# A gated linear attention and two expert layers on one core: elementwise work of GpSimd moved to VectorE, the plan re-costed, heads moved by two queues, and another order of column blocks

## The chip, the core and the metric

One core of one Trainium2 chip runs the whole program. The metric is device microseconds of one execution; a kernel is timed by the median of several executions. The engines are named as the profile names them: PE is TensorE (PEld its weight loads), DVE is VectorE, ACT is ScalarE, POOL is GpSimd, SP is SyncE, which issues most DMAs.

## The reference

The program computes three layers in float32, one after the other:

```python
# attention, B=4, H=8, S=768, D=48
f = 1 / (1 + exp(-f_logit))
for t in range(S):
    state = f[:, :, t, :, None] * state + k[:, :, t] (x) v[:, :, t]   # outer product
    y[:, :, t] = q[:, :, t] @ state
# first expert layer, x: 3072 x 384, hidden width 1536
x = ((x @ w_a) * (x @ w_b)) @ w_out
# second expert layer: 4 experts of width 1024, weighted by normalised probabilities p
out = sum(p[:, e] * (max(x @ w1[e], 0) @ w2[e]) for e in range(4))
```

`w_a`, `w_b` and `w_out` arrive as 64-bit floats and are converted on the chip.

## The kernel before

The attention is done in chunks of 128 time steps: 24 steps, numbered s, for 6 chunks times 4 batches. The decay inside a chunk becomes a running product R (a scan on VectorE, L302). k is multiplied by R (L309) and q divided by it; for the first steps (`early`, s below `EARLY`, 12) the reciprocal is made on ScalarE as exp(-ln R) (L316, L317) and corrected once on VectorE and GpSimd (L318, L320, L322); for the others VectorE divides (L330, four per step) and multiplies (L331). Scores, outputs and state updates are small matmuls (L342, L355, L395, L402, L412). One half of the masked scores goes through VectorE (L371); the other, for early steps after the first four, through a ScalarE copy (L379) and a GpSimd select (L381). The output goes to the tile `xT` as a high and a low part (L432 on ScalarE, L436 on VectorE). Then the heads' last parts are moved to other partitions by six DMAs for each pair of steps (L451, all on SP).

The first expert layer runs over six token blocks of 512 columns and 12 column blocks f of 128 hidden units. A unit (block, f) is nine matmuls for a, nine for b (L500), the product, and the output matmuls: three plain ones for the first ten units (L545, `u < WHOLE`) and nine on split operands for the others (L552). Splitting means that a number is written as a rounded high part plus the low rest: ScalarE rounds (L525, L529), and GpSimd (units below `LATE`, 20) or VectorE subtracts (L532, L535). Each f needs its weights: a 768 KB load, five VectorE operations that turn 64-bit into 32-bit floats (L207, L226, L229, L232, L236), a ScalarE rounding (L250) and a GpSimd subtraction (L254); there are 18 such conversions, 12 for `w_a` and `w_b` and 6 for `w_out`. `ORDER` says which units come first: blocks 0 and 1 take f 0 to 7 each, then f 8 to 11 each. The attention for later blocks is woven in between.

This weaving is done when the program is built. Every operation of these two layers is a `Node` with an engine, a cost in us, what it waits for, and the buffers it takes and gives. A list planner walks through time by these costs and by a few lags (`STRETCH`, `HOP`, `DMA_LAG`) and writes the operations out; each engine then runs its own list strictly in that order. Until the first output matmul the planner fills planned idle time of PE with matmuls on a junk tile (L724). This whole part is called stage A here. Stage B, the second expert layer, follows (L758 and L776); its matmuls need nothing but the weights, which are loaded and split (L127, still on GpSimd), and the token blocks of stage A. `x2` of block 0 is split at the end of stage A (L632).

Of the kernel before, what the change touches and what calls it, by code (L numbers as in the profile page):

```python
# [27 lines left out]
NB = 512  # L28
NBLK = NT // NB
HB = 256  # L30
EARLY = 3 * B

SLOTS = 11
GRP = 2
NSUB = 2
ORDER = ((0, 8, 0), (0, 8, 1), (8, 12, 0), (8, 12, 1))
WHOLE = 10
LATE = 20

T_FIRST, STRETCH, SLACK, PATIENCE, HOP, DMA_LAG = 32.0, 1.15, 1.0, 0.3, 0.06, 2.0  # L40
PRINT = False
LIMIT = float(2.0 ** 60)

# [5 lines left out]
def gla_moe_moe_kernel(ctx: ExitStack, tc, qkf, vv, wab, wout, w12, probs, gq, gv, gp, out):  # L49
# [87 lines left out]
    def phase_a(actx):  # L137
# [30 lines left out]
        def w_plan(u):  # L168
# [24 lines left out]
            if not wide:  # L193
                if out_w:
                    n = Node("ACT", 0.9, lambda: nc.scalar.copy(out=dst(), in_=box["raw"]), [n_f] + guard, give=["k"])
                    w_out_n[f] = w_out_n[f + 1] = n
                    conv_mid.append(n)
                    return
                w, n_w, back = lambda: box["raw"], n_f, ["k"]
            else:  # L200
                seen = wseen[:, u]

                def shift():
                    t = keep.tile([128, 2, 2 * DM], F32, tag="k", name="cv")
# [13 lines left out]

                def exps():
                    return nc.scalar.activation(  # L220
                        out=box["sq"], in_=box["sq"], func=AF.Exp, scale=-64.0 / F64_ZERO, accum_out=seen[:, 1:2]
                    )

                n_s = Node("ACT", 2.2, lambda: (pin(sums()), pin(exps())), [n_f])
                n1 = Node("DVE", 0.8, shift, [n_f, conv_end[-2]], take=["k"])
                n2 = Node("DVE", 1.1, lambda: nc.vector.scalar_tensor_tensor(  # L226
                    out=box["val"].bitcast(U32), in0=box["high"], scalar=0xC0000000, in1=box["mag"].bitcast(U32),
                    op0=ALU.bitwise_and, op1=ALU.bitwise_or), [n1])
                n3 = Node("DVE", 0.72, lambda: nc.vector.tensor_scalar(  # L229
                    out=box["mag"].bitcast(U32), in0=box["val"].bitcast(U32), scalar1=0xFF800000, scalar2=None,  # L230
                    op0=ALU.bitwise_and), [n2])
                n4 = Node("DVE", 1.0, lambda: nc.vector.scalar_tensor_tensor(  # L232
                    out=box["mag"], in0=box["low"], scalar=float(2.0 ** -52), in1=box["mag"], op0=ALU.mult,
                    op1=ALU.mult), [n3])
                conv_mid.append(Node("free", 0.0, None, [n4, n_s], give=["k"]))
                n5 = Node("DVE", 1.0, lambda: nc.vector.tensor_tensor(  # L236
                    out=dst(), in0=box["mag"], in1=box["val"], op=ALU.add), [n4] + guard, give=["k"] if out_w else [])
                if out_w:
                    w_out_n[f] = w_out_n[f + 1] = n5
                    conv_end.append(n5)  # L240
                    return
                w, n_w, back = lambda: box["val"], n5, ["k"]

            def hi():
                if ff == 0:
# [5 lines left out]

            n6 = Node("ACT", 0.83, hi, [n_w] + ([w_n[0]] if ff == 1 else []),
                      take=["x"] if ff == 0 else [] if ff == 1 else ["w"])
            w_n[ff] = Node("POOL", 2.0, lambda: nc.gpsimd.tensor_tensor(  # L254
                out=box["t"][:, 1], in0=w(), in1=box["t"][:, 0].bitcast(F32), op=ALU.subtract), [n6], give=back)
            conv_end.append(w_n[ff])
            if not wide:
# [9 lines left out]
        def step_plan(s):  # L267
# [31 lines left out]
            def scan():  # L299
# [6 lines left out]
            end = slice(C - 1, C)  # L306
            n_max = Node("DVE", 0.15, lambda: dve.tensor_reduce(
                out=flags[:, s, 0:1], in_=t["R"][:, :, C - 1], axis=AX.X, op=ALU.max), [n_R])
            n_k = Node("POOL", 1.6, lambda: pool.tensor_tensor(out=t["k"], in0=t["k"], in1=t["R"], op=ALU.mult),  # L309
                       [n_R, loads["k"]])  # L310

            def new_pe():
# [2 lines left out]
            if early:  # L315
                n = Node("ACT", 0.63, lambda: act.activation(out=t["f"], in_=t["R"], func=AF.Ln), [n_R])  # L316
                n_p = Node("ACT", 0.63, lambda: act.activation(out=t["f"], in_=t["f"], func=AF.Exp, scale=-1.0), [n])  # L317
                n_q = Node("DVE", 1.0, lambda: dve.scalar_tensor_tensor(  # L318
                    out=t["q"], in0=t["q"], scalar=-1.0, in1=t["f"], op0=ALU.mult, op1=ALU.mult), [n_p, loads["q"]])
                n_r = Node("POOL", 1.65, lambda: pool.tensor_tensor(  # L320
                    out=t["R"], in0=t["R"], in1=t["f"], op=ALU.mult), [n_p, n_k, n_max])
                n_q = Node("DVE", 0.75, lambda: dve.scalar_tensor_tensor(  # L322
                    out=t["q"], in0=t["R"], scalar=-2.0, in1=t["q"], op0=ALU.add, op1=ALU.mult), [n_q, n_r])
# [120 lines left out]

            w = GRP * C
            if (o + C) % w == 0:
                def move():
                    z = xT[i].bitcast(F32)[:, :, :, o + C - w:o + C]
                    for h in (0, 64):
                        for kc in range(KC):  # L450
                            dma_i = dma.dma_start(  # L451
                                out=z[h + D:h + 64, :, kc], in_=z[h + 16 * kc:h + 16 * kc + 16, :, 3]
                            )
                            pin(dma_i)
                n_mv = Node("SP", 0.6, move, [lo_n[s], lo_n[s - 1]])
                for d in range(GRP):
                    mv_n[s - d] = n_mv
            if not last:
                def new_state():
                    t["new"] = at.tile([128, 4, D], F32, tag="st", name="st", bufs=B + 1)  # L460
# [22 lines left out]
            else:  # L483
                Node("free", 0.0, None, [n_o, n_pe], give=["st", "pe"])

        x_first, lo_n = {}, {}


        x2ps, x2n, rows, last_op, op_list = {}, {}, [], [None], [None] * 2
# [2 lines left out]
        def unit_plan(u, i, o, n, f, fs):  # L492
# [16 lines left out]
                return nc.scalar.copy(out=t["a"], in_=t["p", 0])  # L509
            n_ac = Node("ACT", 0.59 * narrow, copy_a, [n_a], take=["a"], give=["h"])  # L510
            n_b = state["b"] = Node("PE", cost, lambda: half(1), ready + [n_a], take=["h"])
            eng, cost_l = (nc.vector, "DVE") if u >= LATE else (nc.gpsimd, "POOL")
            if u < WHOLE:
                def mult():
                    t["hl"] = g.tile([128, n], F32, tag="hl", name="hl", bufs=2)
# [2 lines left out]
            else:  # L518
# [8 lines left out]
                def wo_hi():  # L527
# [1 line left out]
                    return nc.scalar.copy(out=t["w"][:, 0], in_=wo_all[:, f])  # L529
                n_m = Node("DVE", 0.69, mult, [n_b, n_ac], take=["ab"], give=["h", "a"])  # L530
                n_h = Node("ACT", 0.61, hl_hi, [n_m], take=["hl"])
                n_h = Node(cost_l, 0.69 if u >= LATE else 1.9, lambda: eng.tensor_tensor(  # L532
                    out=t["hl"][:, 1], in0=t["ab"], in1=t["hl"][:, 0].bitcast(F32), op=ALU.subtract), [n_h], give=["ab"])
                n_w = Node("ACT", 0.51, wo_hi, [w_out_n[f], op_list[-2]], take=["wo"])
                n_w = Node(cost_l, 0.55 if u >= LATE else 1.4, lambda: eng.tensor_tensor(  # L535
                    out=t["w"][:, 1], in0=wo_all[:, f], in1=t["w"][:, 0].bitcast(F32), op=ALU.subtract), [n_w])
                n_h = [n_h, n_w]

# [88 lines left out]
        def split_0(o, lo):  # L627
# [1 line left out]
                x2n["t"] = wts.tile([128, 2, KC, NB], F32R, tag="x", name="x2", bufs=1)  # L629
            t, r = x2n["t"], x2raw[0]  # L630
            if lo:
                return nc.gpsimd.tensor_tensor(  # L632
                    out=t[:, 1, :, o:o + HB], in0=r[:, :, o:o + HB], in1=t[:, 0, :, o:o + HB].bitcast(F32), op=ALU.subtract
                )
            return nc.scalar.copy(out=t[:, 0, :, o:o + HB], in_=r[:, :, o:o + HB])
        n = None
        for o in range(0, NB, HB):
            n = Node("ACT", 0.85, lambda o=o: split_0(o, 0), [state["raw"][0], ahead, n], take=["x"] if o == 0 else [])
            Node("POOL", 2.0, lambda o=o: split_0(o, 1), [n])


        rows[-1][2].append(last_op[0])
# [45 lines left out]
        def finish(x, e):  # L688
# [1 line left out]
            for r in x.give:  # L690
                room[r].append(e)
            for y in users[x]:
                lag = LAG.get(x.eng, 0.0 if x.eng in ("free", y.eng) else HOP)
                at_time[y] = max(at_time[y], e + lag)
                left[y] -= 1
                if not left[y]:
# [345 lines left out]
```

## Time and profile before

| what | value |
|---|---|
| median of 3 runs | 1422.37 us (1420.16 to 1422.44) |
| the profiled execution's own time | 1420.43 us |
| its span, first to last instruction | 1418.7 us |
| PE busy | 1390.8 us, 98% |
| DVE, ACT, POOL busy | 576.4, 419.8, 191.3 us |
| mean granted PE clock | 0.991 |

A matmul's end is modelled in the profile, and the junk matmuls count as busy, so 98% does not say that PE does useful work 98% of the time. The slices of the page show where the other engines are full: DVE is at eight or nine tenths in the first four to five slices of 35 us and at two from the middle on; PE is full from the sixth slice.

### The profile page before, as it was taken

The page shows a single profiled execution, that of the slowest core. Times are in us where ns is not written, and L with a number is a line of the kernel's source. Part 1 is how long each engine was busy: PE and PEld are TensorE (multiplying, and loading weights), DVE is VectorE, ACT ScalarE, POOL GpSimd, SP SyncE. Part 2 cuts the span into 40 slices and gives each one's busy share as a digit, 9 for nine tenths or more (in the row PEclk, how much of TensorE's full clock was granted, in tenths as well). Part 3 has the DMA queues.
Part 4 walks back from the last instruction along what each step waited for, and adds up shares of the span by engine and source line. Part 5 has one row for each costly group of instructions (what it writes and reads, how often), then busy time and mean ns, then how long its engine had stood idle before and what let it go on. Part 6 is the DMA issues. An engine that isn't in the chain of part 4 may idle for free.

```text
span 1418.7 us, 18169 instructions
## 1 busy us (share of the span) xinstructions
PE 1390.8 (98%) x7633; PEld 1187.5 (84%) x7633; DVE 576.4 (41%) x855; ACT 419.8 (30%) x791; POOL 191.3 (13%) x128
## 2 busy tenths in 40 slices
PE   8898899999999999999999999999999999999998
PEld 4576688887888877888999999999989999989997
DVE  8899823647376384532222122222222221222222
ACT  6565534434244343441111211111311112111111
POOL 4243440101000011460000310000400002100000
PEclk9999899999999999999999999999999999999999
DMA  5534201212013021210000110000200001000001
GB/s 203 189 105 153 82 23 36 58 30 74 29 45 93 8 58 40 67 34 0 1 0 1 56 35 0 1 1 0 90 1 0 1 0 38 8 23 23 23 23 47
DMA packets 28169, 60.28 MB, mean 42 GB/s; under 512 B 4016, under 2 KB 9392, under 8 KB 28080
## 3 DMA queue, kind: packets, MB, share of 16 engines
q1 hardware_dynamic: 28080, 59.05, 12.9%
q8 instruction: 62, 1.02, 0.3%
q14 instruction: 27, 0.22, 0.0%
HBM read 51.95 MB, written 4.72 MB: 40 GB/s over the span
## 4 chain that ended last, share of the span: by engine, by line


## 5 line engine op out<-in xcount | busy, mean ns | idle before, releaser
L776 PE MATMUL bank<-w,h 128*128 128x384 f32 x2304 | 411.3, 335 | 0.0
L776 PEld LDWEIGHTS bank<-w,h 128*128 128x128 f32 x2304 | 402.8, 188 | 5.0
L758 PE MATMUL bank<-x,w 128*128 128x512 f32 x1728 | 404.6, 390 | 0.0
L758 PEld LDWEIGHTS bank<-x,w 128*128 128x128 f32 x1728 | 323.4, 188 | 65.1
L761 DVE SCALAR_TENSOR_TENSOR h<-bank,h 128x512 fp32r<-128x512 f32 x192 | 132.8, 692 | 533.2 <-ACT h L760 530.3
L500 PE MATMUL bank<-xT,w 128*128 128x512 f32 (+1 forms) x1332 | 317.8, 392 | 8.8 <-ACT a L509 2.7
L500 PEld LDWEIGHTS bank<-xT,w 128*128 128x128 f32 x1332 | 246.1, 192 | 64.9 <-ACT a L509 3.1
L760 ACT ACTIVATE h<-bank 128x512 fp32r<-128x512 f32 x192 | 115.0, 599 | 615.5 <-PE bank L758 516.3
L552 PE MATMUL bank<-hl,wo 128*128 128x512 f32 x576 | 144.8, 398 | 2.5 <-DVE x2raw L580 2.5
L127 POOL TENSOR_TENSOR w<-raw,w 128x768 fp32r<-128x768 f32 x32 | 59.5, 1862 | 603.5 <-ACT w L126 603.5
L552 PEld LDWEIGHTS bank<-hl,wo 128*128 128x128 f32 x576 | 109.0, 191 | 27.1 <-DVE x2raw L580 3.0
L521 DVE TENSOR_TENSOR ab<-bank,a 128x512 f32<-128x512 f32 x64 | 44.1, 689 | 114.3 <-PE bank L500 88.3
L525 ACT CAST hl<-ab 128x512 fp32r<-128x512 f32 x64 | 39.7, 620 | 110.9 <-DVE ab L521 79.9
L509 ACT COPY a<-bank 128x512 f32<-128x512 f32 (+1 forms) x74 | 42.5, 574 | 95.0 <-PE bank L500 89.2
L532 DVE TENSOR_TENSOR hl<-ab,hl 128x512 fp32r<-128x512 f32 x54 | 49.7, 920 | 39.1 <-ACT hl L525 38.7
L309 POOL TENSOR_TENSOR k<-k,R 128x512 f32<-128x512 f32 x20 | 28.2, 1408 | 266.3 <-DVE R L302 237.1
L786 DVE SCALAR_TENSOR_TENSOR acc<-bank,pr,acc 128x384 f32<-128x384 f32 x72 | 39.5, 610 | 58.6 <-PE bank L776 58.6
L529 ACT CAST wo<-wo_all 128x384 fp32r<-128x384 f32 x64 | 32.7, 512 | 37.4 <-PE bank L552 36.4
L330 DVE RECIPROCAL f<-R 128x128 f32<-128x128 f32 x48 | 42.5, 923 | 0.3
L126 ACT CAST w<-raw 128x768 fp32r<-128x768 f32 x32 | 26.8, 838 | 43.0 <-PE bank L776 30.7
L535 DVE TENSOR_TENSOR wo<-wo_all,wo 128x384 fp32r<-128x384 f32 x54 | 31.5, 583 | 13.8 <-ACT wo L529 13.6
L724 PE MATMUL bank<-junk 128*128 128x512 bf16 x144 | 35.0, 397 | 1.6 <-DVE junk L81 1.6
(109 smaller groups left out, 783.1 us busy)
## 6 DMA issues: line engine op xcount, KB each, us to landing
raw<-in_w_dram SPq DMA_DIRECT2D x32, 384.0 KB, 3.0
raw<-in_wab_dram SPq DMA_DIRECT2D x12, 768.0 KB, 5.2
f<-in_qkf_dram SPq DMA_DIRECT2D x20, 256.0 KB, 2.8
k<-in_qkf_dram SPq DMA_DIRECT2D x20, 256.0 KB, 2.9
q<-in_qkf_dram SPq DMA_DIRECT2D x20, 256.0 KB, 3.2
v<-in_v_dram SPq DMA_DIRECT2D x20, 256.0 KB, 2.9
raw<-in_wout_dram SPq DMA_DIRECT2D x6, 768.0 KB, 7.1
out_dram<-acc SPq DMA_DIRECT2D x24, 192.0 KB, 1.9
```

The source lines that it names most:

```text
L127: engine.tensor_tensor(out=lo, in0=x, in1=hi.bitcast(F32), op=ALU.subtract)
L330: n = Node("DVE", 0.93, lambda j=j: dve.reciprocal(out=t["f"][:, j], in_=t["R"][:, j]), [n])
L500: pin(nc.tensor.matmul(p, l, r, start=m == 0, stop=m == len(ops) - 1))
L509: return nc.scalar.copy(out=t["a"], in_=t["p", 0])
L521: return nc.vector.tensor_tensor(out=t["ab"], in0=t["p", 1], in1=t["a"], op=ALU.mult)
L525: return nc.scalar.copy(out=t["hl"][:, 0], in_=t["ab"])
L532: n_h = Node(cost_l, 0.69 if u >= LATE else 1.9, lambda: eng.tensor_tensor(out=t["hl"][:, 1], in0=t["ab"], in1=t["hl"][:, 0].bitcast(F32), ...
L552: pin(nc.tensor.matmul(banks[m][:, o:o + n], t["w"][:, a, m * 128:(m + 1) * 128], t["hl"][:, b], start=f == fs[0] and q == 0 and o == 0, s ...
L758: nc.tensor.matmul(p, l, r, start=i == 0, stop=i == len(ops) - 1)
L760: nc.scalar.activation(out=h[:, 0], in_=p, func=AF.Relu)
L761: nc.vector.scalar_tensor_tensor(out=h[:, 1], in0=p, scalar=0.0, in1=h[:, 0].bitcast(F32), op0=ALU.max, op1=ALU.subtract)
L776: nc.tensor.matmul(src, h[:, b, t * 128:(t + 1) * 128], w2[e, f][:, a], start=f == 0 and q == 0, stop=f == NF2 - 1 and q == 2,)
```

## The change

Every two-input operation of stage A that GpSimd had goes to VectorE: k times R, R times 1/R, the low parts of the weights, of the products, of `w_out` and of `x2` of block 0. GpSimd keeps the select (L381, now for all steps but the first four) and the splits of stage B. All 24 steps are `early`, so that the VectorE divisions are gone. The planner's costs are the lengths of VectorE operations without a neighbour on GpSimd; `STRETCH` is 1.0, `HOP` 0.08, `DMA_LAG` 1.6. Of the six DMAs that move heads, three are issued by SP and three by ScalarE, each trio planned at 1.95 us. `ORDER` gives blocks 0 and 1 ten column blocks each, then two each.

```diff
-EARLY = 3 * B
+EARLY = NSTEP
-ORDER = ((0, 8, 0), (0, 8, 1), (8, 12, 0), (8, 12, 1))
+ORDER = ((0, 10, 0), (0, 10, 1), (10, 12, 0), (10, 12, 1))
-LATE = 20
-T_FIRST, STRETCH, SLACK, PATIENCE, HOP, DMA_LAG = 32.0, 1.15, 1.0, 0.3, 0.06, 2.0
+T_FIRST, STRETCH, SLACK, PATIENCE, HOP, DMA_LAG = 32.0, 1.0, 1.0, 0.3, 0.08, 1.6
+MOVE = 1.95
+MOVER, MOVER_Q = ("ACT", 1.95), "scalar"
...
-                n1 = Node("DVE", 0.8, shift, [n_f, conv_end[-2]], take=["k"])
+                n1 = Node("DVE", 0.57, shift, [n_f, conv_end[-2]], take=["k"])
...
-            w_n[ff] = Node("POOL", 2.0, lambda: nc.gpsimd.tensor_tensor(
+            w_n[ff] = Node("DVE", 0.97, lambda: nc.vector.tensor_tensor(
...
-            n_k = Node("POOL", 1.6, lambda: pool.tensor_tensor(out=t["k"], in0=t["k"], in1=t["R"], op=ALU.mult),
+            n_k = Node("DVE", 0.69, lambda: dve.tensor_tensor(out=t["k"], in0=t["k"], in1=t["R"], op=ALU.mult),
...
-                n_r = Node("POOL", 1.65, lambda: pool.tensor_tensor(
+                n_r = Node("DVE", 0.69, lambda: dve.tensor_tensor(
...
-                def move():
+                def move(h, queue):
...
-                n_mv = Node("SP", 0.6, move, [lo_n[s], lo_n[s - 1]])
+                n_mv = [
+                    Node("SP", MOVE, lambda: move(0, dma), [lo_n[s], lo_n[s - 1]]),
+                    Node(*MOVER, lambda: move(64, getattr(nc, MOVER_Q)), [lo_n[s], lo_n[s - 1]]),
+                ]
...
-            eng, cost_l = (nc.vector, "DVE") if u >= LATE else (nc.gpsimd, "POOL")
+            eng, cost_l = nc.vector, "DVE"
...
-            Node("POOL", 2.0, lambda o=o: split_0(o, 1), [n])
+            Node("DVE", 0.97, lambda o=o: split_0(o, 1), [n])
```

All lines move down by one to three in the changed kernel (L309 becomes L310, L254 L255, L500 L503, L552 L555, L724 L727). The junk matmuls fall from 144 to 106.

On VectorE, the stretch with the first step of the second chunk (s = 4). Before, what stands there in a row; `cv` is a weight under conversion, `R`, `q`, `pe`, `st` belong to a step, `hl` is the product of a unit:

```order
L232 SCALAR_TENSOR_TENSOR cv<-raw,cv 128x768
L307 TENSOR_REDUCE flags<-R 128x1
L318 SCALAR_TENSOR_TENSOR q<-q,f 128x512
L371 TENSOR_TENSOR ss<-bank_73,mask 128x512
L322 SCALAR_TENSOR_TENSOR q<-R,q 128x512
L324 SCALAR_TENSOR_TENSOR pe<-R,f 128x4
L232 SCALAR_TENSOR_TENSOR cv<-raw,cv 128x768
L236 TENSOR_TENSOR cv<-cv 128x768
```

And in the changed kernel:

```order
L310 TENSOR_TENSOR k<-k,R 128x512
L227 SCALAR_TENSOR_TENSOR cv<-raw,cv 128x768
L308 TENSOR_REDUCE flags<-R 128x1
L319 SCALAR_TENSOR_TENSOR q<-q,f 128x512
L321 TENSOR_TENSOR R<-R,f 128x512
L323 SCALAR_TENSOR_TENSOR q<-R,q 128x512
L325 SCALAR_TENSOR_TENSOR pe<-R,qkf 128x4
L474 SCALAR_TENSOR_TENSOR st<-bank_73,pe 128x192
L230 TENSOR_SCALAR cv<-cv 128x768
L233 SCALAR_TENSOR_TENSOR cv<-raw,cv 128x768
L237 TENSOR_TENSOR cv<-cv 128x768
L255 TENSOR_TENSOR w<-cv,w 128x768
```

The two products with R and the weight's low part (L310, L321, L255) now stand in VectorE's own list, between the conversions.

On PE, the last long run of halves of units before the stretch in which nothing is converted any more. Before (nine matmuls are one half; L552 x3 is a third of a unit's output):

```order
L500 MATMUL bank_68<-xT,w 128x512 x9
L500 MATMUL bank_67<-xT,w 128x512 x9
L412 MATMUL bank_73<-v,kt 64x48 x8
L342 MATMUL bank_72<-ident,k 128x128 x4
...
L552 MATMUL bank_69<-hl,wo 128x512 x3
L552 MATMUL bank_70<-hl,wo 128x512 x3
L552 MATMUL bank_71<-hl,wo 128x512 x3
L395 MATMUL bank_72<-q,st 48x128 x8
L402 MATMUL bank_72<-ss,v 64x128 x8
L500 MATMUL bank_68<-xT,w 128x512 x9
```

And the same place in the changed kernel:

```order
L503 MATMUL bank_67<-xT,w 128x512 x9
L413 MATMUL bank_73<-v,kt 64x48 x8
L343 MATMUL bank_72<-ident,k 128x128 x4
...
L555 MATMUL bank_69<-hl,wo 128x512 x3
L555 MATMUL bank_70<-hl,wo 128x512 x3
L555 MATMUL bank_71<-hl,wo 128x512 x3
L503 MATMUL bank_68<-xT,w 128x512 x9
```

In both the run is seven halves long; ahead of it the changed kernel has four more halves and two more outputs, and the outputs of step 8 (L396, L403) have gone to a later place.

On ScalarE, in the steady stretch of the changed kernel, where the heads are moved:

```order
L512 COPY a<-bank_67 128x512
L433 CAST xT<-bank_72 128x4x128
L451 DMA xT<-xT 16x2x256 x3
L295 ACTIVATE f<-f 128x512
L347 COPY kt<-bank_72 128x512
L380 COPY ss<-bank_74 128x512
L296 ACTIVATE f<-f 128x512
L297 ACTIVATE cap<-f 128x4
L528 CAST hl<-ab 128x512
```

Three DMA issues now stand between a rounding of `xT` and the copies that free the PSUM banks; there are twelve such trios in the program, four of them ahead of the run of seven halves.

## Rows read from the trace of the kernel before

**Rows 1.** Busy time by stage: length, then engines with instructions, PE clock, DMA share, GB/s.

```profile
0.00:168.08 168.08, 149.14 (x968) 101.58 (x968) 152.36 (x190) 100.64 (x208) 65.12 (x47) 0.96 0.44 151
0.00:178.40 178.40, 157.63 (x1016) 108.07 (x1016) 156.80 (x197) 105.85 (x220) 69.39 (x51) 0.94 0.42 145
178.40:617.10 438.70, 437.54 (x2588) 354.25 (x2587) 233.76 (x369) 172.67 (x345) 63.22 (x46) 1.00 0.16 48
617.10:1418.70 801.60, 795.58 (x4034) 725.21 (x4032) 185.88 (x290) 141.24 (x227) 58.74 (x32) 1.00 0.05 17
```

**Rows 2.** PE's timeline: start us, length us, what; in brackets the idle time before.

```profile
48.84 11.61 PE L724 MATMUL bank<-junk 128*128 128x512 bf16 x53
...
154.11 10.06 PE L500 MATMUL bank<-xT,w 128*128 128x512 f32 x36 [2.27 <-DVE ab L521]
...
169.90 6.52 PE L552 MATMUL bank<-hl,wo 128*128 128x512 f32 x15 [2.54 <-DVE x2raw L580]
176.36 1.08 PE L395 MATMUL bank<-q,st 48*48 48x128 f32 x16
...
178.39 8.46 PE L500 MATMUL bank<-xT,w 128*128 128x512 f32 x36
```

**Rows 3.** PE's timeline in the steady stretch.

```profile
545.85 2.20 PE L552 MATMUL bank<-hl,wo 128*128 128x512 f32 x9
547.89 4.24 PE L500 MATMUL bank<-xT,w 128*128 128x512 f32 x18
```

**Rows 4.** DVE groups from 0 to 168.08 us: count, busy us, mean ns, idle before.

```profile
L226 DVE SCALAR_TENSOR_TENSOR cv<-raw,cv 128x768 uint32<-128x768 uint32 x18 | 24.2, 1344 | 0.4
...
L236 DVE TENSOR_TENSOR wo_all<-cv 128x768 f32<-128x768 f32 x6 | 8.9, 1476 | 0.1
```

**Rows 5.** DVE's timeline near the start.

```profile
8.68 1.75 DVE L318 SCALAR_TENSOR_TENSOR qkf<-qkf 128x512 f32<-128x512 f32 x1
10.35 2.29 DVE L302 TENSOR_TENSOR_SCAN R<-qkf,cap 128x512 f32<-128x512 f32 x1
```

**Rows 6.** POOL's timeline at the same place.

```profile
8.05 1.83 POOL L309 TENSOR_TENSOR qkf<-qkf,R 128x512 f32<-128x512 f32 x1 [6.31 <-DMA qkf<-in_qkf_dram]
```

**Rows 7.** DVE instructions by line, whole span: ns min/median/max, first to last start.

```profile
L207 DVE TENSOR_SCALAR cv<-raw x18: 544/552/2198, 7.2 to 160.3; 128x768 uint32<-128x768 uint32 x18
L226 DVE SCALAR_TENSOR_TENSOR cv<-raw,cv x18: 947/959/2520, 7.8 to 160.8; 128x768 uint32<-128x768 uint32 x18
L302 DVE TENSOR_TENSOR_SCAN R<-f,cap x20: 1207/1216/1227, 67.3 to 517.3; 128x512 f32<-128x512 f32 x20
L331 DVE TENSOR_TENSOR q<-q,f x12: 679/682/693, 265.7 to 523.2; 128x512 f32<-128x512 f32 x12
L521 DVE TENSOR_TENSOR ab<-bank,a x64: 628/692/693, 144.1 to 611.4; 128x512 f32<-128x512 f32 x64
L535 DVE TENSOR_TENSOR wo<-wo_all,wo x54: 533/554/2193, 221.9 to 614.6; 128x384 fp32r<-128x384 f32 x54
```

**Rows 8.** DVE groups of the whole span, two of the short operations.

```profile
L307 DVE TENSOR_REDUCE flags<-R 128x1 f32<-128x4 f32 x24 | 3.6, 152 | 0.2
...
L73 DVE MEMSET cap<- 128x512 f32 x1 | 0.5, 485 | 1.0 <-PEq L1031 1.0
```

**Rows 9.** POOL group from 0 to 168.08 us.

```profile
L381 POOL TENSOR_SCALAR_AFFINE_SELECT ss<-ss 128x512 f32<-128x512 f32 x5 | 5.1, 1023 | 10.6 <-ACT ss L379 10.6
```

**Rows 10.** SP's timeline: the first six DMAs that move heads.

```profile
28.82 3.92 SPq L451 DMA_DIRECT2D xT<-xT  x6
```

**Rows 11.** DMA issues: count, KB each, median us to landing.

```profile
xT<-xT SPq DMA_DIRECT2D x72, 32.0 KB, 2.0
```

**Rows 12.** Busy time in a slice of 5 us, columns as in the first group.

```profile
170.00:175.00 5.00, 5.00 (x12) 3.95 (x13) 1.21 (x3) 1.56 (x3) 2.66 (x3) 0.50 0.31 98
```

**Rows 13.** ACT group from 178.4 to 617.1 us.

```profile
L509 ACT COPY a<-bank 128x512 f32<-128x512 f32 x60 | 35.2, 587 | 81.0 <-PE bank L500 78.8 <-DVE R L302 1.9 <-DVE ab L521 0.2
```

**Rows 14.** PE's waits from 178.4 to 617.1 us: us in total, times, longest.

```profile
PE bank L500 <- DMA xT<-xT: 0.9, 1, 0.9
```

More of the change, by code (lines that the diff above doesn't have):

```diff
@@ L224, in w_plan @@
                 n_s = Node("ACT", 2.2, lambda: (pin(sums()), pin(exps())), [n_f])
-                n1 = Node("DVE", 0.8, shift, [n_f, conv_end[-2]], take=["k"])
-                n2 = Node("DVE", 1.1, lambda: nc.vector.scalar_tensor_tensor(
+                n1 = Node("DVE", 0.57, shift, [n_f, conv_end[-2]], take=["k"])
+                n2 = Node("DVE", 0.97, lambda: nc.vector.scalar_tensor_tensor(
                     out=box["val"].bitcast(U32), in0=box["high"], scalar=0xC0000000, in1=box["mag"].bitcast(U32),
                     op0=ALU.bitwise_and, op1=ALU.bitwise_or), [n1])
-                n3 = Node("DVE", 0.72, lambda: nc.vector.tensor_scalar(
+                n3 = Node("DVE", 0.57, lambda: nc.vector.tensor_scalar(
                     out=box["mag"].bitcast(U32), in0=box["val"].bitcast(U32), scalar1=0xFF800000, scalar2=None,
                     op0=ALU.bitwise_and), [n2])
-                n4 = Node("DVE", 1.0, lambda: nc.vector.scalar_tensor_tensor(
+                n4 = Node("DVE", 0.97, lambda: nc.vector.scalar_tensor_tensor(
                     out=box["mag"], in0=box["low"], scalar=float(2.0 ** -52), in1=box["mag"], op0=ALU.mult,
@@ L235, in w_plan @@
                 conv_mid.append(Node("free", 0.0, None, [n4, n_s], give=["k"]))
-                n5 = Node("DVE", 1.0, lambda: nc.vector.tensor_tensor(
+                n5 = Node("DVE", 0.97, lambda: nc.vector.tensor_tensor(
                     out=dst(), in0=box["mag"], in1=box["val"], op=ALU.add), [n4] + guard, give=["k"] if out_w else [])
@@ L317, in step_plan @@
                 n_p = Node("ACT", 0.63, lambda: act.activation(out=t["f"], in_=t["f"], func=AF.Exp, scale=-1.0), [n])
-                n_q = Node("DVE", 1.0, lambda: dve.scalar_tensor_tensor(
+                n_q = Node("DVE", 0.69, lambda: dve.scalar_tensor_tensor(
                     out=t["q"], in0=t["q"], scalar=-1.0, in1=t["f"], op0=ALU.mult, op1=ALU.mult), [n_p, loads["q"]])
-                n_r = Node("POOL", 1.65, lambda: pool.tensor_tensor(
+                n_r = Node("DVE", 0.69, lambda: dve.tensor_tensor(
                     out=t["R"], in0=t["R"], in1=t["f"], op=ALU.mult), [n_p, n_k, n_max])
-                n_q = Node("DVE", 0.75, lambda: dve.scalar_tensor_tensor(
+                n_q = Node("DVE", 0.69, lambda: dve.scalar_tensor_tensor(
                     out=t["q"], in0=t["R"], scalar=-2.0, in1=t["q"], op0=ALU.add, op1=ALU.mult), [n_q, n_r])
@@ L446, in step_plan @@
             if (o + C) % w == 0:
-                def move():
+                def move(h, queue):
                     z = xT[i].bitcast(F32)[:, :, :, o + C - w:o + C]
[L449 to L454, printed above, removed]
-                n_mv = Node("SP", 0.6, move, [lo_n[s], lo_n[s - 1]])
+                    for kc in range(KC):
+                        pin(queue.dma_start(
+                            out=z[h + D:h + 64, :, kc], in_=z[h + 16 * kc:h + 16 * kc + 16, :, 3]
+                        ))
+                n_mv = [
+                    Node("SP", MOVE, lambda: move(0, dma), [lo_n[s], lo_n[s - 1]]),
+                    Node(*MOVER, lambda: move(64, getattr(nc, MOVER_Q)), [lo_n[s], lo_n[s - 1]]),
+                ]
+                movers.append(n_mv[1])
                 for d in range(GRP):
-                    mv_n[s - d] = n_mv
+                    mv_n[s - d] = Node("free", 0.0, None, n_mv)
             if not last:
@@ L484, in step_plan @@
                 Node("free", 0.0, None, [n_o, n_pe], give=["st", "pe"])
-        x_first, lo_n = {}, {}
+        x_first, lo_n, movers = {}, {}, []
         x2ps, x2n, rows, last_op, op_list = {}, {}, [], [None], [None] * 2
@@ L531, in unit_plan @@
                 n_h = Node("ACT", 0.61, hl_hi, [n_m], take=["hl"])
-                n_h = Node(cost_l, 0.69 if u >= LATE else 1.9, lambda: eng.tensor_tensor(
+                n_h = Node(cost_l, 0.69, lambda: eng.tensor_tensor(
                     out=t["hl"][:, 1], in0=t["ab"], in1=t["hl"][:, 0].bitcast(F32), op=ALU.subtract), [n_h], give=["ab"])
                 n_w = Node("ACT", 0.51, wo_hi, [w_out_n[f], op_list[-2]], take=["wo"])
-                n_w = Node(cost_l, 0.55 if u >= LATE else 1.4, lambda: eng.tensor_tensor(
+                n_w = Node(cost_l, 0.5, lambda: eng.tensor_tensor(
                     out=t["w"][:, 1], in0=wo_all[:, f], in1=t["w"][:, 0].bitcast(F32), op=ALU.subtract), [n_w])
@@ L631, in split_0 @@
             if lo:
-                return nc.gpsimd.tensor_tensor(
+                return nc.vector.tensor_tensor(
                     out=t[:, 1, :, o:o + HB], in0=r[:, :, o:o + HB], in1=t[:, 0, :, o:o + HB].bitcast(F32), op=ALU.subtract
@@ L692, in finish @@
             for y in users[x]:
-                lag = LAG.get(x.eng, 0.0 if x.eng in ("free", y.eng) else HOP)
+                lag = (LAG["SP"] if x in movers else LAG.get(x.eng, 0.0 if x.eng in ("free", y.eng) else HOP))
                 at_time[y] = max(at_time[y], e + lag)
```

## The prediction

> **What bounds the kernel now.** Busy time by stage comes first, to find where PE lacks work. Stage B takes 801.6 us of 1418.7, and from 178.4 us to its start PE is busy 437.54 of 438.70 us [rows 1]. In the steady stretch one matmul run follows another: nine L552 from 545.85, the next start at 547.89 [rows 3], so 2.04 / 9 = 0.2267 us each. From 178.4 us on the program is PE's work and nothing else. So the end is the moment at which PE becomes full, plus the work that it has left then: 1420.43 - 178.4 = 1242.0 us of the profiled execution's own time.
>
> Ahead of that moment PE is short of work, although the windows show 157.63 us busy of 178.40: matmuls on junk count, as in the run of 53 that takes 11.61 us [rows 2]. Of the work that has to be done, the matmuls in PE's list up to that place make about 115 us at the lengths of [rows 3]. So some 64 us are lost, all of it early, and only there can the change gain.
>
> Next the engine that holds PE up there. The last weight conversion ends at 168.08 us, and up to it VectorE is busy 152.36 us, 91% [rows 1], more than any other engine that PE waits for. PE's waits end with VectorE: 2.27 us before 154.11, 2.54 us before 169.90 [rows 2]. So the moment at which PE becomes full is that at which VectorE is through with the conversions and what stands between them.
>
> Then, why VectorE takes so long. L226 has a median of 959 ns over the program and a mean of 1344 in this stretch; L236, of the same size, has 1476 [rows 4, 7]. The timeline of the two engines shows when: L318 starts at 8.68 and takes 1.75 us while GpSimd's L309 runs from 8.05 to 9.88 [rows 5, 6]; an operation of the same size alone takes 0.68 (L331) [rows 7]. GpSimd is busy 65.12 us of the stretch [rows 1], nearly all of it with the two-input operations that the change removes.
>
> **VectorE's list, costed anew.** I count VectorE's list of the changed kernel up to the low part of `w_out` that the last run of halves needs (its 234th instruction), by lengths without a neighbour [rows 7, 8]:
> - 18 conversions: L207 and L229 at 0.55, L226, L232 and L236 at 0.96, 3.98 each: 71.6.
> - 12 low parts of weights, 0.96: 11.5, new.
> - 9 steps: scans 1.22, 11.0; four products of 128x512 each at 0.68 (k and R new): 24.5.
> - 32 operations of that size that read PSUM (the masks L371, the low parts of `xT`, L521), 0.69: 22.1.
> - low parts of `hl` and `wo`, five each, 0.68 and 0.55: 6.2, new.
> - 44 short ones, 0.15 (L307) to 0.49 (L73): 11.1.
>
> The sum is 158.0 us. New in it are k and R 12.4, low parts 11.5 + 6.2, and 3.1 of products, a mask and copies that now stand earlier: 33.2. Without them the old list makes 124.8 us, where the trace has 152.36: 27.6 us are stretching by GpSimd. **VectorE gives up 27.6 and takes on 33.2**, 5.6 us more than before. That alone would be a loss.
>
> **What PE has done by then.** The gain is in the other term. At that place of its list PE has done, in the changed order, four halves more (36 L500, 8.2 us at 0.2267) and two outputs more (18 L552, 4.1), and step 8's outputs less (176.36 to 178.39, 2.0) [rows 2, 3]. Each weight column is used by two blocks, so with ten columns by turns instead of eight there is more for PE to do with what is converted. That leaves 10.2 us less behind the place. So PE may become full 10.2 us later than 178.4, at 188.6, for no change.
>
> **The sum.** Idle time of VectorE up to its last conversion is 168.08 - 152.36 = 15.7 us [rows 1], 5.7 of it before the first data; I keep it. 158.0 + 15.7 = 173.7 us, 14.9 ahead of 188.6. The profiled execution would end at 1420.4 - 14.9 = 1405.5 us. The median of the runs is 1.9 above that execution: **1407**.
>
> The rest of the change I cost at nothing, and this is the cover of each:
> - Movers. SP issues six in 3.92 us [rows 10]; three each by two queues are 1.96, and the data land after 2.0 as before [rows 11]. The first pair of blocks has its heads 1.9 us sooner, which lies inside the idle time kept; loads queued on SP behind them start that much sooner too. On ScalarE the four trios of the early part are 7.8 us of an engine busy 100.64 of 168.08 [rows 1]; without that slack the copies behind them free PE's banks late (a rival). PE waits for moved heads once later on, 0.9 us [rows 14].
> - Selects. GpSimd still runs five in this part, 1.02 us each [rows 9], 5.1 in all. The trace shows none beside a VectorE operation apart from others, so they cost between 0 and 5.1; I take 0, since a select reads one tensor and L318 was held by a GpSimd operation that reads two.
> - Reciprocals. 48 divisions are gone, but behind 178.4, where VectorE is busy 233.76 of 438.70; what moves there from GpSimd takes half or less of its old time, and fits. `x2` of block 0 is split while PE still has whole units to do.
> - Junk. 38 fewer take nothing from PE's work.
> - The planner's constants only set the order that I counted. Stage B's matmuls, loads and splits stay: 801.6.
>
> New waits in VectorE's list: k's product waits for a DMA, each low part for ScalarE's rounding, and behind them queue L521 and L371, for which PE waits. They are in the idle time; bounds are below.
>
> **Bounds.** Neighbours overlap a little: 8.68 + 1.75 is 10.43, the next starts at 10.35 [rows 5]. At half of 233 places 0.08 us is 9.3 less: 1397. Upward, 5.1 for selects and as much again for waits: 1417. The forecast's own range is 1397 to 1417.
>
> **Rivals.**
> A. *VectorE idles 15 us more.* Each step and each low part now goes VectorE, ScalarE, VectorE in strict order; before, GpSimd did the last leg. 12 low parts, 18 step products and 5 of `hl` are 35 places; at 0.43 us each the gain is gone: 1422. For it: VectorE's list is 91% full and a late input can't be passed. Against it: the order puts other conversions between a rounding and its low part.
>
> B. *The movers stop PE late.* Behind 178.4, ScalarE's L509 copies free PE's banks and have 81.0 us idle before 60 of them, 1.35 each [rows 13]. A trio takes 1.96, waits for VectorE's low part of `xT` (0.69) and, if the queue must land an earlier transfer first, 2.0: 4.65, or 3.3 beyond the slack. Eight trios lie there: 26.4 us, 1407 + 26 = 1433, slower. It decides from 14.9 / 8 = 1.9 us per trio. Against it: the six on SP show 0.65 each with no landing between them [rows 10], and PE has several banks to go on with.
>
> C. *The clock.* The granted clock is 0.96 in this part and was 0.50, the lower level, in 170 to 175 after PE had waited 2.54 us [rows 1, 2, 12]; a 5 us stretch at 1.2 GHz loses 2.5. Four more of these, since PE has 38 junk matmuls fewer, are 10 us: 1417. The Trainium skill, "TensorE: Matmul & The Clock Gate", Part 1, says that the slow state is the default and that activity lifts it; fewer junk matmuls would by that cost clock, and the slice at 0.50 agrees with it.
>
> D. *The stretching stays*, so the change doesn't do what it says: VectorE's operations are long for another reason, such as the DMA load of these 170 us, 0.44 [rows 1]. Then 27.6 us come on top: full at 201.3, 12.7 after the break-even, 1435, slower. Against it: from 178.4 on GpSimd is busy 63.22 of 438.70 and the medians are the short lengths [rows 1, 7]. The Trainium skill, "Perfetto Trace Analysis", section "Optimizing Scalar/DVE Operations", says that a saturated VectorE may gain by giving work to ScalarE or GpSimd, which speaks against the change, and adds that the two share a read port, so that moving work between them might not help. By the first half VectorE's added work comes on top of its old time, which is this rival and its 1435; by the second the stretching goes and the sum above stands. The trace agrees with the second where L318 and L309 meet [rows 5, 6].
>
> **How the numbers follow.** 0.2%, 2.8 us, is about what a measurement of this kernel tells from no change. Forecast 0.70 and C 0.09 are faster, 0.79. A: 0.09, the same. B 0.06 and D 0.06 are slower, 0.12. The range runs from the forecast's low end to A's: 1397 to 1421.
>
> **What would show it.** Right: in the early part the means of L227 and L237 fall to about 0.96 us and that of L319 to 0.7; VectorE is busy near 158 us before the last low part of `w_out` in the early run; PE is full from about 174; the last stage is 801.6. Wrong: VectorE's means above 1.2 us (D); the means short but VectorE idle over 25 us (A); PE waiting in the steady stretch for ScalarE's copies behind L451 (B); slices of half clock more than now (C). If PE is full at 174 and the time isn't near 1407, the count of PE's work is wrong.

## The result and the profile after

The changed kernel takes 1397.3 us (median of 4, 1396.56 to 1398.95); the kernel before, beside it, 1421.6. The ratio is 0.9832, 95% interval 0.9815 to 0.9849: 24 us or 1.7% faster. The forecast was 1407 with a range from 1397 to 1421, so the direction holds, the range holds by 0.3 us at its low end, and the gain is 24 us where 14.9 was worked out.

| what | before | after |
|---|---|---|
| the profiled execution's own time | 1420.43 us | 1396.56 us |
| start of stage B, the bound of the windows | 617.1 us | 593.2 us |
| length of stage B | 801.6 us | 801.6 us |
| PE idle in the first 200 us | 21.0 us | 10.3 us |
| junk matmuls, and their time | 144, 35.0 us | 106, 28.0 us |
| granted PE clock in the first 200 us | 0.95 | 0.98 |

Busy time by stage, after; the columns are those of [rows 1].

```profile
0.00:163.10 163.10, 152.85 (x1000) 108.75 (x1001) 145.48 (x236) 105.41 (x219) 5.17 (x13) 0.98 0.45 157
0.00:178.40 178.40, 168.16 (x1067) 121.44 (x1068) 155.32 (x252) 112.69 (x233) 5.17 (x13) 0.98 0.42 148
178.40:593.20 414.80, 412.48 (x2497) 334.55 (x2496) 211.23 (x348) 185.44 (x367) 33.09 (x25) 1.00 0.16 50
593.20:1394.80 801.60, 795.64 (x4034) 725.22 (x4032) 186.00 (x290) 141.26 (x227) 58.73 (x32) 1.00 0.05 16
```

Stage B has its old length to the tenth, so the whole gain lies ahead of it. Up to stage B PE is idle 12.6 us in place of 21.9, 9.4 less; junk takes 7.0 us less; and the other matmuls, as many as before, take 7.5 us less, where the granted clock of the first 200 us is 0.98 in place of 0.95. Together that is 23.9 us.

VectorE's groups up to 163.1 us, after. They answer to [rows 4], where the first two had 1344 and 1476 ns.

```profile
L227 DVE SCALAR_TENSOR_TENSOR cv<-raw,cv 128x768 uint32<-128x768 uint32 x18 | 16.9, 950 | 0.2
...
L255 DVE TENSOR_TENSOR w<-cv,w 128x768 fp32r<-128x768 f32 x12 | 11.4, 951 | 1.1 <-ACT w L251 1.1
...
L237 DVE TENSOR_TENSOR wo_all<-cv 128x768 f32<-128x768 f32 x6 | 5.7, 950 | 0.0
...
L319 DVE SCALAR_TENSOR_TENSOR q<-q,f 128x512 f32<-128x512 f32 x5 | 3.4, 689 | 0.9 <-ACT f L318 0.9
```

The stretching is gone: these groups stand at their length alone. But PE's timeline, with the end of VectorE's last conversion below it, speaks against the picture that the forecast made of it:

```profile
122.91 2.34 PE L503 MATMUL bank<-xT,w 128*128 128x512 f32 x9 [1.15 <-DVE hl L519]
...
136.04 4.24 PE L503 MATMUL bank<-xT,w 128*128 128x512 f32 x18
...
142.16 14.44 PE L503 MATMUL bank<-xT,w 128*128 128x512 f32 x63
```

```profile
155.98 0.95 DVE L237 TENSOR_TENSOR wo_all<-cv 128x768 f32<-128x768 f32 x1
```

The wait of 1.15 us ahead of 122.91 is PE's last before 237 us. VectorE ends its last conversion at 156.93, 33 us later, and in those 33 us PE never waits. In the old kernel [rows 2] its waits came up to 170.

### The profile page after: what moved, and what is told of

Same layout as the page of the kernel before. It is cut to its first block, busy times and chain, and to the rows that moved or that the text cites. A ratio compares the mean times of both kernels' runs of the same rounds, so it can differ in the third digit from the quotient of the medians.

```text
span 1394.8 us, 18018 instructions
## 1 busy us (share of the span) xinstructions
PE 1376.3 (99%) x7595; PEld 1181.2 (85%) x7595; DVE 552.6 (40%) x889; ACT 439.4 (32%) x827; POOL 97.0 (7%) x70
## 3 DMA queue, kind: packets, MB, share of 16 engines
q1 hardware_dynamic: 26352, 57.87, 12.5%
## 4 chain that ended last, share of the span: by engine, by line
## 5 line engine op out<-in xcount | busy, mean ns | idle before, releaser
L503 PE MATMUL bank<-xT,w 128*128 128x512 f32 (+1 forms) x1332 | 317.9, 390 | 7.9 <-DVE hl L519 5.4
L503 PEld LDWEIGHTS bank<-xT,w 128*128 128x128 f32 x1332 | 244.5, 189 | 62.3 <-DVE hl L519 6.4
L555 PE MATMUL bank<-hl,wo 128*128 128x512 f32 x576 | 143.3, 395 | 0.0
L555 PEld LDWEIGHTS bank<-hl,wo 128*128 128x128 f32 x576 | 108.5, 190 | 23.8 <-issue 0.3
L535 DVE TENSOR_TENSOR hl<-ab,hl 128x512 fp32r<-128x512 f32 x64 | 55.4, 865 | 33.1 <-ACT hl L528 32.9
L382 POOL TENSOR_SCALAR_AFFINE_SELECT ss<-ss 128x512 f32<-128x512 f32 x20 | 18.0, 899 | 489.4 <-ACT ss L380 291.1
L538 DVE TENSOR_TENSOR wo<-wo_all,wo 128x384 fp32r<-128x384 f32 x64 | 35.4, 554 | 15.3 <-ACT wo L532 15.3
L727 PE MATMUL bank<-junk 128*128 128x512 bf16 x106 | 28.0, 413 | 1.6 <-DVE junk L82 1.6
L303 DVE TENSOR_TENSOR_SCAN R<-f,cap 128x512 f32<-128x512 f32 x20 | 25.6, 1282 | 6.5 <-ACT cap L297 5.5
```

What stands on the lines that cost most here:

```text
L503: pin(nc.tensor.matmul(p, l, r, start=m == 0, stop=m == len(ops) - 1))
L535: n_h = Node(cost_l, 0.69, lambda: eng.tensor_tensor(out=t["hl"][:, 1], in0=t["ab"], in1=t["hl"][:, 0].bitcast(F32), op=ALU.subtract), [n_ ...
L555: pin(nc.tensor.matmul(banks[m][:, o:o + n], t["w"][:, a, m * 128:(m + 1) * 128], t["hl"][:, b], start=f == fs[0] and q == 0 and o == 0, s ...
```

## The experiments

Every variant is planned anew when it is built, so each shows an edit together with the order that the planner then writes. Differences below are between medians; the changed kernel's is 1397.3. The ratios are to the kernel before on the same chip, whose medians were 1419.7 to 1421.6. Most intervals reach about 2.5 us to either side, so a difference of less than about 3 us between two variants is not told from none.

| variant | us | ratio, 95% interval | last conversion ends, us |
|---|---|---|---|
| before | 1419.7 to 1421.6 | 1 | 168.1 |
| before, ten column blocks alone | 1422.95 | 1.0019 (1.0008 to 1.0030) | 168.8 |
| before, VectorE takes GpSimd's work alone | 1421.95 | 1.0011 (0.9999 to 1.0024) | 168.1 |
| before, ten, movers | 1413.73 | 0.9952 (0.9935 to 0.9968) | 166.6 |
| before, ten, movers, planner's numbers | 1413.52 | 0.9950 (0.9934 to 0.9967) | 161.0 |
| after | 1397.3 | 0.9832 (0.9815 to 0.9849) | 156.9 |
| after, eight column blocks | 1407.03 | 0.9901 (0.9880 to 0.9923) | 156.3 |
| after, GpSimd has its work again | 1406.31 | 0.9904 (0.9885 to 0.9923) | 160.5 |
| after, only the weights' low parts on GpSimd | 1403.75 | 0.9879 (0.9860 to 0.9897) | 157.9 |
| after, twelve early steps | 1402.93 | 0.9884 (0.9858 to 0.9909) | 158.6 |
| after, old stretch, hop and lag | 1401.80 | 0.9873 (0.9856 to 0.9889) | 158.0 |
| after, movers all on SP | 1397.81 | 0.9838 (0.9821 to 0.9856) | 162.0 |
| after, first masks by ScalarE and GpSimd | 1397.98 | 0.9839 (0.9821 to 0.9856) | 158.3 |
| after, twelve column blocks | 1394.45 | 0.9811 (0.9793 to 0.9829) | 145.1 |

**The order, undone.**

```diff
-ORDER = ((0, 10, 0), (0, 10, 1), (10, 12, 0), (10, 12, 1))
+ORDER = ((0, 8, 0), (0, 8, 1), (8, 12, 0), (8, 12, 1))
```

> The changed kernel with the old order of column blocks (eight by turns, then four). Theory (two gains that add up: 10.2 us of PE work put ahead of the moment at which VectorE is through, the rest from VectorE being through sooner): VectorE passes its last conversion within 3 us of where it does in the changed kernel (157 us), PE has about 10 us less done by then, and the time is 1407, between 1404 and 1411. Rival 1 (the order does nothing, VectorE's work is all): 1397 to 1400. Rival 2 (the order is the whole gain): 1418 to 1422.

Measured 1407.0, 9.7 more, as the theory had it. How it comes about is another matter. PE's timeline, then VectorE's, of this variant:

```profile
145.40 0.60 PE L343 MATMUL bank<-ident,k 128*128 128x128 f32 x4
151.73 2.08 PE L356 MATMUL bank<-q,k 48*128 48x128 f32 x16 [5.74 <-DVE q L323]
```

```profile
148.26 0.96 DVE L237 TENSOR_TENSOR cv<-cv 128x768 f32<-128x768 f32 x1
149.14 0.68 DVE L321 TENSOR_TENSOR R<-R,f 128x512 f32<-128x512 f32 x1
149.74 0.35 DVE L466 TENSOR_TENSOR st<-bank,st 128x192 f32<-128x192 f32 x1
150.12 0.96 DVE L255 TENSOR_TENSOR w<-cv,w 128x768 fp32r<-128x768 f32 x1
151.00 0.68 DVE L323 SCALAR_TENSOR_TENSOR q<-R,q 128x512 f32<-128x512 f32 x1
```

One step's products (L321, L323) stand in VectorE's list among the operations of the conversions, PE's list has no unit at this place, and PE waits 5.74 us for the second of them. With ten by turns the run of seven halves at 142.16 covers this stretch of conversions. Most of the order's gain is one long wait avoided, with the half clock behind it (the scores take 2.08 us there at a granted clock of 0.50; 1.16 at full clock); another 3.4 us is junk, 31.4 us in this variant against 28.0.

**The order alone.** The kernel before with the line of ten by turns.

> The kernel before with the new order of column blocks alone (ten by turns, then two); GpSimd keeps all its work. Theory: the order is worth its 10.2 us also here, since VectorE's list up to its last conversion hardly changes: 1411, between 1408 and 1415, with VectorE's operations stretched as before (L226 mean above 1.3 us up to the last conversion). Rival (the order pays only where VectorE is faster, because here PE waits for each new column block anyway): 1419 to 1422.

Measured 1422.95, slower by 2.4 than the kernel before beside it: the rival's side, 1 us above its range. PE's timeline:

```profile
48.06 1.33 PE L500 MATMUL bank<-xT,w 128*128 128x256 f32 x9
49.24 17.23 PE L724 MATMUL bank<-junk 128*128 128x512 bf16 x79
70.93 4.28 PE L500 MATMUL bank<-xT,w 128*128 128x256 f32 x21 [4.46 <-DVE hl L516]
...
160.16 5.02 PE L500 MATMUL bank<-xT,w 128*128 128x512 f32 x14 [3.49 <-DMA xT<-xT]
```

and VectorE's, ahead of the product for which PE waits at 70.93:

```profile
66.50 0.56 DVE L229 TENSOR_SCALAR cv<-cv 128x768 uint32<-128x768 uint32 x1
67.10 0.96 DVE L232 SCALAR_TENSOR_TENSOR cv<-raw,cv 128x768 f32<-128x768 uint32 x1
68.09 2.45 DVE L236 TENSOR_TENSOR cv<-cv 128x768 f32<-128x768 f32 x1
70.46 0.41 DVE L516 TENSOR_TENSOR hl<-bank,a 128x256 f32<-128x256 f32 x1
```

PE had ended the halves at 49.4. The product L516 that frees their bank, 0.41 us of work, starts at 70.46, behind the conversions of later columns, one of them stretched to 2.45. The old planner had planned PE idle there, and filled the time with 79 junk matmuls. The kernel before has the same place with 53 [rows 2]. At 160.16 PE waits for heads that six DMAs on one queue move.

**GpSimd's work given back** to the changed kernel: the engines and costs of L255, L310, L321, L535 and L538 as before; the split of `x2` stays on VectorE.

> The changed kernel with every two-input operation of the first part given back to GpSimd (k times R, R times 1/R, low parts of weights, of the products and of w_out of the first twenty units); order, movers, early steps and constants stay changed. Theory: VectorE's operations are stretched again (mean of the L227 conversion stage above 1.25 us against 0.95) and the time is the changed kernel's plus what does not belong to the order, 24.3 - 10.2 = 14 us: 1411, between 1405 and 1417. Rival (the stretching is covered and the gain is from order, movers and constants): 1396 to 1400.

Measured 1406.3, 9.0 more, less than the 14 of the theory but in its range. VectorE's groups up to 170 us:

```profile
L227 DVE SCALAR_TENSOR_TENSOR cv<-raw,cv 128x768 uint32<-128x768 uint32 x18 | 25.3, 1405 | 0.4
...
L208 DVE TENSOR_SCALAR cv<-raw 128x768 uint32<-128x768 uint32 x18 | 16.4, 909 | 0.0
```

The stretching is back. VectorE's timeline at its last conversion:

```profile
159.57 0.95 DVE L237 TENSOR_TENSOR cv<-cv 128x768 f32<-128x768 f32 x1
```

It ends at 160.5, 3.6 us later than in the changed kernel, and the program ends 9 us later. PE is idle 21.8 us of the first 200, against 10.3.

**The weights' low parts alone** on GpSimd:

```diff
-w_n[ff] = Node("DVE", 0.97, lambda: nc.vector.tensor_tensor(
+w_n[ff] = Node("POOL", 2.0, lambda: nc.gpsimd.tensor_tensor(
```

> The changed kernel with the twelve low parts of the weights alone back on GpSimd. They take 11.5 us off VectorE's list and hold up what runs beside them. Theory (break-even: in the run with everything given back the conversion stages L208 and L227 were 0.33 and 0.45 us longer in the mean, 14 us over 18 conversions): 1396 to 1401. Rival A (these carry the 9 us that giving everything back cost): 1404 to 1408. Rival B (the relief counts more than the stretching): 1388 to 1394.

Measured 1403.75, 6.5 more: nearest to rival A, some 70% of the cost of giving all back. VectorE's timeline, GpSimd's and PE's:

```profile
57.24 0.95 DVE L237 TENSOR_TENSOR wo_all<-cv 128x768 f32<-128x768 f32 x1
...
58.86 2.40 DVE L227 SCALAR_TENSOR_TENSOR cv<-raw,cv 128x768 uint32<-128x768 uint32 x1
...
62.96 0.95 DVE L237 TENSOR_TENSOR cv<-cv 128x768 f32<-128x768 f32 x1
63.83 0.42 DVE L519 TENSOR_TENSOR hl<-bank,a 128x256 f32<-128x256 f32 x1
```

```profile
58.27 2.17 POOL L255 TENSOR_TENSOR w<-cv,w 128x768 fp32r<-128x768 f32 x1 [7.14 <-ACT w L251]
```

```profile
53.22 1.33 PE L503 MATMUL bank<-xT,w 128*128 128x256 f32 x9 [1.55 <-ACT a L512]
64.30 2.07 PE L503 MATMUL bank<-xT,w 128*128 128x256 f32 x8 [9.75 <-DVE hl L519]
```

L227 ends 0.8 us after GpSimd's operation at 60.44, about its own length: it had stood still as long as GpSimd ran. But the one wait of 9.75 us is for a product behind conversions again; PE had ended its halves at 54.6.

**The move to VectorE alone**, in the kernel before.

> The kernel before with the move from GpSimd to VectorE alone; column blocks, movers, early steps and the planner's other numbers as before. My prediction's sum without its term for the order: 4.7 us less than before, 1415 to 1418. Theory P (the move needs the rest: the loss between 40 and 70 us belongs to the planner's numbers and stays, and for steps after the twelfth the product k times R now queues on VectorE behind four reciprocals, so that PE waits in the stretch where it was full): 1417 to 1426, with PE waiting for L310 or its line after 230 us. Rival (freeing VectorE of the stretching pays by itself): 1408 to 1413.

Measured 1421.95: no change, with no stretching left (L226 mean 973 ns). The worst place, PE's timeline and VectorE's:

```profile
161.88 1.11 PE L342 MATMUL bank<-ident,k 128*128 128x128 f32 x4 [7.98 <-DVE k L309]
```

```profile
159.28 0.96 DVE L232 SCALAR_TENSOR_TENSOR cv<-raw,cv 128x768 f32<-128x768 uint32 x1
160.27 0.96 DVE L236 TENSOR_TENSOR cv<-cv 128x768 f32<-128x768 f32 x1
161.14 0.68 DVE L309 TENSOR_TENSOR k<-k,R 128x512 f32<-128x512 f32 x1
```

The product k times R is now one of VectorE's list, behind conversions. The wait that was expected at the reciprocals came earlier, at conversions. Over the first 200 us PE is idle 27.1 us, against 21.0 in the kernel before, at a granted clock of 0.93 against 0.95: what the stretching cost came back as such waits.

**Early steps.** `EARLY = 3 * B` in the changed kernel.

> The changed kernel with twelve early steps as before, so that VectorE makes the 48 reciprocals of the later steps again (some 42 us of VectorE's time after PE is full). Theory: they lie beside a full PE: 1396 to 1400. Rival (in VectorE's strict order they delay the products and the planner's early part changes with them): 1403 or more.

Measured 1402.9, 5.6 more: the rival's side. VectorE's timeline and PE's:

```profile
240.13 2.56 DVE L331 RECIPROCAL f<-R 128x128 f32<-128x128 f32 x3
242.62 0.62 DVE L437 TENSOR_TENSOR xT<-bank,xT 128x512 fp32r<-128x512 f32 x1
243.16 0.94 DVE L331 RECIPROCAL f<-R 128x128 f32<-128x128 f32 x1
244.02 0.62 DVE L310 TENSOR_TENSOR k<-k,R 128x512 f32<-128x512 f32 x1
```

```profile
244.70 1.12 PE L343 MATMUL bank<-ident,k 128*128 128x128 f32 x4 [3.44 <-DVE k L310]
```

In the stretch where PE was full, k times R queues behind four reciprocals, and PE waits 3.44 us; the granted clock from 240 to 250 us is 0.72, where the changed kernel has 0.83. Part of the 5.6 lies earlier: PE is idle 12.5 us of the first 200, against 10.3. In the kernel before, that product was GpSimd's and passed them.

**The planner's numbers.** Stretch, hop and lag of before in the changed kernel.

> The changed kernel with the planner's old stretch 1.15, hop 0.06 and DMA lag 2.0; the node costs stay changed. My prediction's step (these numbers only set an order that hardly matters for the sum): 1396 to 1400. Theory P (they set where the products stand in VectorE's list, which is what the early part loses by): PE loses 8 us or more beyond the changed kernel between 30 and 125 us: 1405 to 1417.

Measured 1401.8, 4.5 more. PE's timeline and VectorE's:

```profile
64.44 4.21 PE L503 MATMUL bank<-xT,w 128*128 128x512 f32 x9 [4.27 <-DVE hl L519]
```

```profile
63.10 0.95 DVE L237 TENSOR_TENSOR cv<-cv 128x768 f32<-128x768 f32 x1
63.97 0.42 DVE L519 TENSOR_TENSOR hl<-bank,a 128x256 f32<-128x256 f32 x1
```

L519, for which PE waits, starts at 63.97 behind conversions. The theory's sign holds; its size is less than expected.

**Movers, and movers with the planner's numbers,** in the kernel before with ten by turns. Two runs.

> The kernel before with the new order of column blocks and the movers of the change (three on SyncE, three on ScalarE, planned at 1.95 us each with the landing added); GpSimd, early steps and the planner's other numbers as before. In the run with the order alone PE waited 5.4 us for moved heads, and loses 26 us between 40 and 70 us, where VectorE's list has the first units' products (L516) behind the conversions of later columns. Theory P (the planner's costs put the products there): the waits on moved heads go, the loss between 40 and 70 stays, 1416 to 1421. Theory M (the late movers of the old plan are the cause, and the planner plans around them): 1403 to 1411.

> As the run before it, with the changed planner's numbers too: stretch 1.0, hop 0.08, DMA lag 1.6, and the five conversion operations at their lengths alone; GpSimd keeps its two-input work and the first twelve steps alone are early. Theory P: the first units' products come between the conversions, the loss between 40 and 70 us falls from 26 to under 10 us, and the time is that of the run with everything given back to GpSimd: 1404 to 1410. Theory M or early steps as the cause: 1415 or more.

Measured 1413.73 and 1413.52. The movers are worth 9.2 there, more than the first theory gave and less than the second; PE's waits for moved heads fall from 5.4 to 0.9 us. The planner's numbers add nothing, against what I expected: junk falls from 177 to 101 matmuls (42.7 to 25.9 us), but PE's idle time rises from 14.6 to 23.4 in the first 200 us, with 4.35 us for a product L525:

```profile
160.14 5.79 PE L504 MATMUL bank<-xT,w 128*128 128x512 f32 x18 [4.35 <-DVE ab L525]
```

The waits on heads account for 4.5 of the 9.2. Beside that the matmuls other than junk take 4.4 us less up to stage B, at a granted clock of 0.98 against 0.96 in the first 200 us; why the clock is higher isn't settled, nor how the gain divides between the second queue and the planned length.

**Movers back on SP** in the changed kernel, planned as two nodes of 1.95.

> The changed kernel with all six DMAs that move heads on SyncE again, as two nodes of three. Theory: they lie on no path once the first units run; the first pair of blocks gets its heads 1.9 us later, so 1397 to 1400. Rival A (two queues are worth 1.9 us for each of the four early pairs): 1403 to 1406. Rival B (the issues cost ScalarE more than they give): 1392 to 1395.

Measured 1397.8: within 0.5. VectorE's last conversion:

```profile
161.00 0.95 DVE L237 TENSOR_TENSOR wo_all<-cv 128x768 f32<-128x768 f32 x1
```

It ends 5 us later than in the changed kernel, and the time is the same.

**Masks of the first steps.** `if s < EARLY:` for the copy and the select.

> The changed kernel with one mask of each of the first four steps too as a ScalarE copy and a GpSimd select instead of a VectorE product: 4 x 0.68 = 2.7 us off VectorE's list in the first 40 us, 2.4 on ScalarE. If VectorE's list sets PE's lost time there: 1394 to 1396. If the chain of each step does (VectorE, ScalarE, PE by turns), the longer chain costs: 1397 to 1402.

Measured 1398.0, no difference that can be told; so 2.7 us off VectorE's list gave nothing. The conversions did not end sooner either (158.3).

**Twelve by turns.**

> The changed kernel with all twelve column blocks of block 0 first, then all of block 1. Theory (the order pays because block 1's units run on columns that are already converted while the last ones are converted; with twelve by turns no unit of block 1 covers the last three conversions, some 15 us of VectorE): PE waits for w or hl longer between 100 and 150 us, 1400 to 1410. Rival (more by turns is simply better, as ten against eight was): 1390 to 1396.

Measured 1394.45: the theory is wrong, and the rival has it. VectorE's last conversion:

```profile
144.12 0.95 DVE L237 TENSOR_TENSOR wo_all<-cv 128x768 f32<-128x768 f32 x1
```

It ends 11.9 us sooner than in the changed kernel, and the time is 2.9 less. The intervals of the two ratios overlap, so that it beats the changed kernel is likely but not shown.

## Why the prediction was right, and where not

**The stretching** was read rightly. L227 and L237 are at 0.95 us, L319 at 0.69, and the two runs that give work back have it again (L227 1405 and 1141 ns). One reading was too broad: the 1476 ns of L236 are those of its six for `w_out`, and the other twelve had 983 in the kernel before. The Trainium skill, "SBUF — State Buffer", section "SBUF: two separate sides", says that the port pair which VectorE and GpSimd share is locked whole for one instruction, by a GpSimd operation or by certain VectorE operations, among them those with two inputs in SBUF, whichever starts first, while the other waits. L227 at 58.86 above, 2.40 us beside GpSimd's 2.17, agrees. Rival D falls with it.

**VectorE's sum**: the lengths were right, the sum was not. I had 158.0 us busy and 15.7 idle, 173.7. Measured at the place that I counted to (163.1): 145.5 busy and 17.6 idle. The term that I sized wrongly is the overlap of neighbours: the lengths in the trace (count times mean of each group) add up to some 159 us over 236 instructions, so about 14 us is overlap, 0.06 each. I took it as nothing in the sum and put 9.3 in the range. With the measured moment the same sum gives 163.1 - 188.6 = -25.5, and the two profiled executions differ by 23.9. But PE waits nowhere between 124 and 237 us, so the count of its work would fit at any place in that stretch; the fit does not show that VectorE sets the moment.

**The step that failed** is "the moment at which PE becomes full is that at which VectorE is through with the conversions". PE is full from 124, where the sum had 174, and VectorE is through at 156.9. Over the variants of the changed kernel that keep ten by turns the end of the last conversion doesn't set the time: 157.9 goes with 1403.75, 160.5 with 1406.3, 162.0 with 1397.8. What the traces show at PE's long waits instead is a short operation that frees a bank or feeds PE (L519, L310, L323) behind conversions or reciprocals in VectorE's strict list. Each is a wait of 3 to 10 us, or the junk planned for it, and some bring half clock. No run moves such an operation by itself, so that these places make up the whole of PE's lost time is argued and not shown.

**The order's 10.2** came out at 9.7 when undone in the changed kernel, and at -2.4 alone in the kernel before. My term was a count of PE's work at one place; what it buys depends on whether a long wait stands there to be covered.

**The move alone** has 4.7 us in my sum. It is worth 0 alone and 9.0 in the changed kernel. By the Trainium skill, "Perfetto Trace Analysis", section "Optimizing Scalar/DVE Operations", moving work between these two engines might not help; by themselves the runs agree (ratio 1.0011), and with the rest of the change they don't.

**What I costed at nothing.** The movers' queue: right, 0.5 in the changed kernel; but in the kernel before with ten by turns, two queues planned at their real length are worth 9.2. The reciprocals: wrong, 5.6; the cover that I named, a full PE, ends where k times R moves into the same list, and PE waits 3.44 us there. The planner's constants ("only set the order that I counted"): wrong, 4.5. The selects: nearly right. GpSimd's timeline after has two of five longer than 0.64:

```profile
111.44 1.02 POOL L382 TENSOR_SCALAR_AFFINE_SELECT ss<-ss 128x512 f32<-128x512 f32 x1 [13.53 <-ACT ss L380]
123.68 1.14 POOL L382 TENSOR_SCALAR_AFFINE_SELECT ss<-ss 128x512 f32<-128x512 f32 x1 [11.21 <-ACT ss L380]
```

VectorE's timeline beside them:

```profile
111.89 0.60 DVE L325 SCALAR_TENSOR_TENSOR pe<-R,f 128x4 f32<-128x4 f32 x1
...
124.24 0.99 DVE L208 TENSOR_SCALAR cv<-raw 128x768 uint32<-128x768 uint32 x1
```

One L325 takes 0.60 instead of 0.16 and one L208 0.99 instead of 0.55, 0.9 us together of the 5.1 that I had as the bound.

**The rivals.** A: VectorE idles 17.6 us, not 30. B: PE never waits for ScalarE's copies after 124. C: the clock rose from 0.95 to 0.98 with fewer junk matmuls and 10.7 us less PE idle time in the first 200.

So the gain of 24 us isn't a sum of parts. Undone one at a time they cost 9.7 (order), 9.0 (GpSimd), 5.6 (early steps), 4.5 (planner) and 0.5 (movers), 29.3 together; the first two, done alone, give nothing. The forecast's 14.9 was worked out from two of them, and lay low with the overlap, the early steps and the planner's numbers costed at nothing. That the range holds is in part luck: its low end, 0.3 us under the measured time, was set by overlap in VectorE's list, whose end doesn't set the time. How the 9.0 divides into stretching and list order stays open, since each variant is planned anew.

## What to carry to other kernels

An engine that is 90% busy for a while need not be the bound: ask for each wait of the bottleneck which single instruction ends it, and what stands ahead of that one in its engine's list. When work moves onto an engine that runs strictly in order, its own length is not all: look at what it now queues behind and what queues behind it; in one run PE went without work for 21 us until a product of 0.41 us had its turn. And costs given to a planner are part of the kernel: re-measure them when an engine's neighbours change.

## What the hardware showed unexpectedly

Neighbouring VectorE operations overlap by 0.06 us in the mean, about 14 us over 236 instructions: more than the 9.3 that a single pair in the trace [rows 5] had suggested for half of the places. GpSimd's select of one tensor, taken as free, has a price: where two of the first five took 1.02 and 1.14 us instead of 0.64, a VectorE operation beside each was 0.44 us longer than alone.
